# Moving the low parts of w1 from GpSimd to VectorE, one slice later, in a fused attention and two-MoE kernel

## The chip, the cores and the metric

The kernel runs on one core of one Trainium2 chip. The metric is the device time of one execution in microseconds (us). Five engines of the core work beside each other, each through its own instructions in order: TensorE (PE; its weight loads are shown as PEld), VectorE (DVE), ScalarE (ACT), GpSimd (POOL) and SyncE (SP), which issues most DMAs. An instruction starts when those ahead of it on its engine are through and the semaphores it waits for have been raised.

## The reference

Three layers follow each other. Only the second one matters here.

```python
x = attention(q, k, v)                      # 4 x 768 tokens, 512 wide: 3072 rows
logits = x @ w_gate                         # 8 experts
for idx in argsort(-logits.flatten()):      # greedy: best pair of token and expert first
    tok, e = divmod(idx, 8)
    if assigned[tok] >= 0 or counts[e] >= 384: continue
    assigned[tok] = e; counts[e] += 1
for e in range(8):                          # 384 tokens for each expert
    out[assigned == e] = relu(x[assigned == e] @ w1[e]) @ w2[e]
return soft_moe(out, phi, m2w1, m2w2)       # 32 slots, softmax over tokens and over slots
```

`w1[e]` is 512 x 1024 and `w2[e]` 1024 x 512, all in float32.

## The kernel before

**Stages.** After the attention the kernel finds, by a search, which expert fills first and with which 384 tokens, then the next, and so on: eight stages `r` = 0 to 7, one expert each. Here stage r.s means step s of stage r. While stage r multiplies, the search for later stages runs beside it.

**A step.** Stage r has 8 steps `fc`, one for each slice of 128 columns of w1. A step's product (`mm1`, L1251) is made of 12 matmuls of 128x384: x and w1 are both split into a high part in float32r and a low part (the rest), and high times high, high times low of x, and low of w1 times high are added. ScalarE then applies the relu (`hT`, L1262), and TensorE transposes (`turn_h`, L1272). `dispatch(r - 1)`, a generator, adds pieces of the finished stage's work at the ends of the steps: its fifth piece, at the end of step 4, multiplies by the first half of w2 (`pS`, L1430) and then issues the loads of the second half (`weights2`, L1240), since w2 has two buffers; the second half of `pS` stands at the end of step 6.

**Weights of a step.** SyncE loads a slice of w1 into `raw` (L1202, 256 KB, 4 buffers). ScalarE copies it, rounded, into `wh` (L1216), and GpSimd subtracts, `wl = raw - wh` (L1218; VectorE only for the first two slices of all). Both have 3 buffers. At the start of step k, `split` makes wh and wl of slice k + 2, and `fetch` issues the load of slice k + 6, which goes into the `raw` that slice k + 2 has used: SyncE waits there until that slice's wl is made. SyncE's other loads (w2, `pr`, and `mw`, the weights of the third layer) stand behind in the same queue.

**Other work of GpSimd** in these stages: three gathers of token rows for the next stage (L1171), and three scatters for the last (L1308).

**The search** (`_assign_rounds`) goes round by round, six digits each, back and forth between VectorE and TensorE. In the profile's lines: VectorE compares (`G`, L760) and prepares (`D1`, L767); TensorE counts (`A`, L791); VectorE casts (L800); TensorE picks (`B`, L803); VectorE (L814); TensorE adds (`C`, L816); VectorE (L819) and again L760. After the last digit VectorE makes `B_r` (L827), TensorE sums (`M`, L830 and L831), VectorE decides in nine small operations (L833 to L852), TensorE makes offsets (`o`, L700 and L701), and VectorE goes on (L856 to L869). `T` (L625) places tokens.

**What sets the order.** All engines follow the order in which the code is written. Where the search's instructions fall among the others is set by a running estimate: each matmul adds its cost to `pe` in `tick`; when `pe` reaches the time at which VectorE's answer should be ready, `advance` writes the search's next instructions, for TensorE and VectorE, at that place. `search_state["dve"]` estimates when VectorE is free; `other` adds VectorE work that isn't the search's. The subtraction on GpSimd does not stand in it.

Of the kernel before, what the change touches and what calls it, by code (L numbers as in the profile page):

```python
# [10 lines left out]
F32 = mybir.dt.float32  # L11
# [5 lines left out]
ALU = mybir.AluOpType  # L17
# [898 lines left out]
def tile_kernel(  # L916
# [13 lines left out]
    nc = tc.nc  # L930
# [17 lines left out]
    search_state = {"pe": 0.0, "dve": 0.0, "ready": 1e18, "cost": 0.0, "done": False, "stage": -1, "placed": set()}  # L948
# [204 lines left out]
    with ExitStack() as c2:  # L1153
        wp = c2.enter_context(tc.tile_pool(name="wp", bufs=2))

        XG, EI, ER, W, W2, PR, RAW = {}, {}, {}, {}, {}, {}, []
# [34 lines left out]
        def low_x():  # L1191

            dc, pt = LOW.pop(0)
            nc.vector.tensor_tensor(X[:, 1, dc], pt, X[:, 0, dc].bitcast(F32), ALU.subtract)
            other(480)

        def fetch(k):

            while len(RAW) <= k and len(RAW) < 8 * E and len(RAW) // 8 in EI:
                r, u = divmod(len(RAW), 8)  # L1200
                raw = ring.tile([128, 4, 128], F32, name=f"raw{r}_{u}", tag="raw", bufs=NRAW)
                nc.sync.dma_start(  # L1202
                    raw,
                    w1[bass.ds(number(r), 1), :, 128 * u : 128 * u + 128].rearrange("o (c p) f->p (o c) f", p=128),
                )
                RAW.append(raw)

        def split(k):

            fetch(k)  # L1210
            while len(W) <= k and len(W) < len(RAW):
                r, u = divmod(len(W), 8)
                raw = RAW[len(W)]
                wh = ring.tile([128, 4, 128], F32R, name=f"wh{r}_{u}", tag="wh", bufs=NWHL)
                wl = ring.tile([128, 4, 128], F32R, name=f"wl{r}_{u}", tag="wl", bufs=NWHL)
                nc.scalar.copy(wh, raw)  # L1216

                (nc.gpsimd if r or u > 1 else nc.vector).tensor_tensor(wl, raw, wh.bitcast(F32), ALU.subtract)  # L1218
                W[8 * r + u] = (wh, wl)

        def fetch_p(r):
            pr = wp.tile([128, 8, 32], F32, name=f"pr{r}", tag="pr", bufs=1)
            nc.sync.dma_start(
                pr.rearrange("p c s->p (c s)"), pd[bass.ds(number(r), 1), :, :].rearrange("o p s->p (o s)")
            )
            PR[r] = pr
# [233 lines left out]
        def part(t, i):  # L1460
            return lambda name: [t[:, 1024 * i : 1024 * i + 1024]]
# [21 lines left out]
        with tc.manual_schedule(engines=engines | {mybir.EngineType.Activation}):  # L1483
            for r in range(E):
                search_state["stage"] = r
                if r:
                    fetch_p(r)
                fill = dispatch(r - 1) if r else iter(())
                next(fill, None)
                for fc in range(8):  # L1490
                    split(8 * r + fc + NWHL - 1)
                    fetch(8 * r + fc + NWHL - 1 + NRAW)
                    if r == 0 and fc == 1:
                        fetch_p(r)
                    ahead = fc == 7 and r + 1 in XG
                    if ahead:
                        mm1(r, 7, (lambda: None, lambda: transpose_x(r + 1, 0), lambda: transpose_x(r + 1, 1), low_x))
                    elif fc == 4:
                        mm1(r, 4, (lambda: None, lambda: logits(r, 0)))
                    elif r == E - 1 and fc in (2, 3):  # L1500
                        mm1(r, fc, (lambda: None, lambda: next(fill)))
                    else:
                        mm1(r, fc)
                    if r == E - 1 and fc == 7:
                        logits(r, 1, range(3))
                    if fc == 2:
                        next(fill, None)
                    while turned < 8 * r + fc - (2 if 8 * r + fc < 8 * E - 3 else 1) + 1:
                        turn_h(*divmod(turned, 8))
                        turned += 1  # L1510
                    if ahead:
                        low_x()
                    if fc >= 3 and r + 1 in PLACED and r + 1 not in XG:
                        gather(r + 1)
                    if r == E - 1 and fc == 5:
                        weights2(r, (2, 3))
                    if fc != 2:
                        next(fill, None)
                    while early and NPRE - len(early) < (NPRE * (8 * r + fc)) // 56:
                        load_pieces(early.pop(0))  # L1520
                    if search_state["done"] and not late:
                        right.close()
                        late.append(right.enter_context(tc.tile_pool(name="late", bufs=NLATE, side="right")))
                        later += NLATE * [slot(late[0], "mw")]
                    if later and fc % 2:
                        load_pieces(later.pop())
                    if r == E - 1 and fc == 1:
                        load_pieces(part(xp.tile([128, 1536], F32, name="xg_mw", tag="xg"), 0))
                    if r == E - 1 and fc >= 6:
                        load_pieces(halves(ring, ("wh", "wl"), NWHL))  # L1530
                for _ in fill:
                    pass
                if r + 1 < E:
                    while r + 1 not in PLACED:
                        advance()
                    if r + 1 not in XG:
                        gather(r + 1)
                        until = search_state["pe"] + 5000
                        while search_state["ready"] < until:
                            advance()  # L1540
                        search_state["pe"] = max(search_state["pe"], until)
                    for dc in range(4):
                        if dc > 1 or not ahead:
                            transpose_x(r + 1, dc)
                            if len(LOW) > 1:
                                low_x()
                    while LOW:
                        low_x()
                    logits(r, 1)
                else:  # L1550
                    logits(r, 1, (3,))
                    turn_h(r, 7)
                    filler(r, 1)
            x = xp.tile([128, 3072], F32, name="x_mw", tag="x")
            load_pieces(halves(ring, ("wh", "wl"), NWHL), *[part(x, i) for i in range(3)])
            for _ in dispatch(E - 1):
                pass
            load_pieces(*2 * [slot(ring, "w2", 2)], *2 * [halves(ring, ("raw", "raw"), NRAW)])
# [200 lines left out]
```

## Time and profile before

| | us |
|---|---|
| median of 3 runs | 572.71 (572.52 to 573.27) |
| the profiled execution, its own time | 575.3 |
| its span, first to last instruction | 573.6 |
| stage 0 begins | 235.2 |
| stages 1, 2, 3, 4, 5, 6, 7 begin | 266.2, 303.0, 338.9, 376.6, 409.9, 441.7, 473.7 |
| last product of stage 7 ends | 500.2 |

The 1.7 us between span and time lie around the instructions. In the span TensorE is busy 93%, VectorE 60%, ScalarE 55%, GpSimd 38%. A row of a timeline gives the start and the duration in us, the engine, the line, the operation, what it writes and reads, shapes, and in square brackets how long the engine sat idle ahead of it and what ended that. Records of matmuls overlap: the next one starts before the record of the one ahead ends.

### The profile page before, as it was taken

To read this page: it belongs to the slowest core of one execution; us is meant where nothing else is said; L and a number is where in the kernel's file an instruction comes from. 1 tells how busy PE (TensorE), PEld (TensorE's weight loads), DVE (VectorE), ACT (ScalarE), POOL (GpSimd) and SP (SyncE) were. 2 spreads that over 40 slices of the span, in tenths; PEclk is the share of its full clock that TensorE was granted. 3 is DMA by queue.
4 is the path that set the end of the run, shared out by engine and by line. 5 is a ranking of instruction groups with operands and counts; after the bars stand their busy time and mean duration, and the time that the engine had idled before them with its cause. 6 is when DMAs were issued, how large, how long until landed. Compare 5 with 4: busy or idle time off the path is not lost.

```text
span 573.6 us, 15062 instructions
## 1 busy us (share of the span) xinstructions
PE 531.9 (93%) x5765; PEld 387.8 (68%) x5765; DVE 342.4 (60%) x1115; ACT 315.9 (55%) x670; POOL 219.0 (38%) x264
## 2 busy tenths in 40 slices
PE   4889999999998999998999999999999989979994
PEld 3676877777776766677667676677677767753473
DVE  5688987959845576879778897573423213031242
ACT  2778887878755766544536354455464535421231
POOL 3666554536410003153362554625465553421000
PEclk9999999999999999999999999999999999999998
DMA  9997896995865994355284674856859895789997
GB/s 188 202 192 185 221 193 160 250 232 167 311 209 193 392 332 147 102 169 171 94 289 147 200 252 127 264 173 208 281 160 342 252 338 170 250 260 370 357 346 215
DMA packets 157795, 130.64 MB, mean 228 GB/s; under 512 B 43332, under 2 KB 128964, under 8 KB 157724
## 3 DMA queue, kind: packets, MB, share of 16 engines
q1 hardware_dynamic: 151916, 115.26, 70.1%
q0 software_dynamic: 4368, 13.37, 7.3%
q10 hardware_dynamic: 1440, 1.05, 0.6%
q8 instruction: 46, 0.75, 0.6%
q14 instruction: 25, 0.20, 0.1%
HBM read 113.98 MB, written 14.02 MB: 223 GB/s over the span
## 4 chain that ended last, share of the span: by engine, by line
PE 61%; DVE 19%; DMA 6%; ACT 5%; issue 4%; POOL 3%; another core or an unknown queue 1%; SPq 0%; POOLq 0%; DVEq 0%; ACTq 0%
PE ph L1251 15%; DMA w<-in_moe_w_dram 5%; PE pwt L1049 4%; PE pp L1014 3%; PE po L1710 3%; PE pS L275 3%; PE po L313 3%; PE mh L1647 2%; PE pS L1430 2%; PE pt L1272 2%; DVE G_r L760 2%; PE l L1292 2%; PE pA L1325 2%; PE pf L1669 2%; PE pv L177 2%
## 5 line engine op out<-in xcount | busy, mean ns | idle before, releaser
L1251 PE MATMUL ph<-x,wh 128*128 128x384 f32 x512 | 145.6, 360 | 0.0
L1218 POOL TENSOR_TENSOR wl<-raw,wh 128x512 fp32r<-128x512 f32 x62 | 82.6, 1334 | 132.7 <-ACT wh L1216 104.4
L1251 PEld LDWEIGHTS ph<-x,wh 128*128 128x128 f32 x512 | 88.6, 189 | 22.2 <-issue 20.3
L1251 PE MATMUL ph<-x,wl 128*128 128x384 f32 x256 | 88.5, 346 | 0.0
L1262 ACT ACTIVATE hT<-ph 128x384 f32<-128x384 f32 x64 | 31.2, 488 | 74.7 <-PE ph L1251 63.2
L292 POOL TENSOR_TENSOR X<-X,mn 128x480 f32<-128x480 f32 x48 | 47.3, 985 | 64.2 <-DVE mn L288 40.2
L1251 PEld LDWEIGHTS ph<-x,wl 128*128 128x128 f32 x256 | 48.1, 188 | 0.0
L1171 POOL DMA_INDIRECT xg<-xd,ids x24 | 23.2, 968 | 61.6 <-PE pwt L1049 52.4
L287 DVE TENSOR_TENSOR X<-pS,nm 128x480 f32<-128x480 f32 x48 | 31.3, 651 | 14.8 <-PE pS L275 14.2
L1216 ACT CAST wh<-raw 128x512 fp32r<-128x512 f32 x64 | 39.9, 623 | 0.0
L1064 ACT COPY wt<-pwt 128x512 f32<-128x512 f32 x60 | 33.1, 591 | 11.8 <-PE pwt L1049 10.5
L221 ACT COPY kT<-pk 64x384 f32<-64x384 f32 x62 | 31.4, 507 | 9.8 <-PE pk L206 9.0
L1049 PE MATMUL pwt<-ident,pw 128*128 128x128 f32 x224 | 33.6, 281 | 1.1 <-ACT wt L1064 0.6
L296 ACT ACTIVATE X<-X 128x480 f32<-128x480 f32 x48 | 29.3, 610 | 8.4 <-POOL X L292 7.6
L1272 PE MATMUL pt<-ident,hT 128*128 128x128 f32 x192 | 33.9, 277 | 0.0
L275 PE MATMUL pS<-kwin,qT 64*64 64x120 f32 x768 | 32.1, 276 | 1.8 <-POOL kwin L243 1.8
L1274 ACT COPY h<-pt 128x384 f32<-128x384 f32 x64 | 30.2, 474 | 6.1 <-PE pt L1272 5.8
L288 DVE TENSOR_REDUCE mn<-X 128x4 f32<-128x480 f32 x48 | 31.3, 653 | 3.7
L275 PEld LDWEIGHTS pS<-kwin,qT 64*64 64x64 f32 x768 | 28.1, 138 | 5.0 <-POOL kwin L243 2.4
L1308 POOL DMA_INDIRECT cd<-ce,ids x24 | 24.5, 1020 | 17.5 <-DVE den L1422 13.6
L313 PEld LDWEIGHTS po<-vw,AT 120*64 120x64 f32 x768 | 24.9, 137 | 8.6 <-issue 3.1
L760 DVE TENSOR_TENSOR G_r<-D_r,as_cn 128x768 bf16<-128x768 bf16 (+1 forms) x41 | 29.2, 713 | 1.2
(293 smaller groups left out, 1062.1 us busy)
## 6 DMA issues: line engine op xcount, KB each, us to landing
mw<-in_moe_w_dram SPq DMA_DIRECT2D x55, 512.0 KB
raw<-in_moe_w_dram SPq DMA_DIRECT2D x64, 256.0 KB
w<-in_moe_w_dram SPq DMA_DIRECT2D x30, 512.0 KB
pw<-in_moe_w_dram SPq DMA_DIRECT2D x28, 512.0 KB
vw<-in_v_dram SPq DMA_DIRECT2D x32, 240.0 KB
kt<-in_k_dram SPq DMA_DIRECT2D x32, 192.0 KB
qt<-in_q_dram SPq DMA_DIRECT2D x32, 192.0 KB
xd<-xb POOLq DMA_DIRECT2D x4, 1536.0 KB
```

What stands on the lines that cost most here:

```text
L221: lambda r, d, s: nc.scalar.copy(d, s) if n or r else nc.vector.tensor_copy(d, s),
L275: nc.tensor.matmul(PS[n][i][64 * u : 64 * u + 64, j, :], qT[r, 64 * T : 64 * T + 64], kwin[r, T, :], start=True, stop=True,)
L287: nc.vector.tensor_tensor(X, PS[n][i], nm[:, i // 2], ALU.add)
L292: nc.gpsimd.tensor_tensor(X, X, MN.pop((n, i))[:, :, None].to_broadcast([128, 4, 120]), ALU.subtract)
L313: nc.tensor.matmul(PO[n][T // 6][64 * (T % 2) : 64 * (T % 2) + 64, T // 2 % 3, hh, :], AT[n, i][0:120, j, 64 * u : 64 * u + 64], vw[0:120, ...
L760: v.tensor_tensor(G, Dg.rearrange("p (q j)->p q j", j=J)[:, :, None, :].to_broadcast([128, 24 // J, n, J]), C["cn", n][:, None].to_broadca ...
L1049: nc.tensor.transpose(pt[:, dc], PW[e, q][t][:, 128 * dc : 128 * dc + 128], ident)
L1064: nc.scalar.copy(wt[:, :, 128 * t : 128 * t + 128], pt)
L1216: nc.scalar.copy(wh, raw)
L1218: (nc.gpsimd if r or u > 1 else nc.vector).tensor_tensor(wl, raw, wh.bitcast(F32), ALU.subtract)
L1251: nc.tensor.matmul(ph, a[:, dc], b[:, dc], start=dc == n == 0, stop=(dc, n) == (3, 2),)
L1272: nc.tensor.transpose(pt[:, c], HT[r, fc][:, 128 * c : 128 * c + 128], ident)
```

## The change

The subtraction of slice k + 2 is no longer issued with its copy. `split` puts it on a list, `WL`, and `low_w`, called at the start of each step, ahead of `split`, takes the oldest entry and issues it on VectorE. So at the start of step k VectorE gets wl of slice k + 1, and the copy of slice k + 2 follows on ScalarE. The first two slices are done at once, as before. Each call adds 600 ns to the estimate of VectorE. GpSimd keeps the gathers and scatters. Lines behind the edit are higher by 10 or 11 (L1251 is then L1261, L1430 is L1440, L1240 is L1250; the subtraction is L1228).

```diff
                 nc.scalar.copy(wh, raw)
-
-                (nc.gpsimd if r or u > 1 else nc.vector).tensor_tensor(wl, raw, wh.bitcast(F32), ALU.subtract)
                 W[8 * r + u] = (wh, wl)
+                WL.append((wl, raw, wh))
+                if r == 0 and u < 2:
+                    low_w()
+
+        WL = []
+
+        def low_w():
+
+            if WL:
+                wl, raw, wh = WL.pop(0)
+                nc.vector.tensor_tensor(wl, raw, wh.bitcast(F32), ALU.subtract)
+                search_state["dve"] = max(search_state["dve"], search_state["pe"] + 196) + 600
...
                 for fc in range(8):
+                    low_w()
                     split(8 * r + fc + NWHL - 1)
```

TensorE before, from the end of 1.4 into 1.5 (`ph1_4` and `ph1_5` are the products of the two steps, `pt` a transpose, `pS0` the first half of the second product, `as` the search's bank):

```order
L830 MATMUL as_3045<-as_w23_483,as_on_487 128x8
L831 LDWEIGHTS as_o32_319
L831 MATMUL as_3045<-B_r3_4964,as_o32_319 128x8
L1251 MATMUL ph1_4_4954<-x_3023,wl1_4_4792 128x384
L1251 MATMUL ph1_4_4954<-x_3023,wh1_4_4791 128x384 x2
L1251 MATMUL ph1_4_4954<-x_3023,wl1_4_4792 128x384
L1272 MATMUL pt1_2_5004<-ident_66,hT1_2_4836 128x128 x3
L1430 MATMUL pS0_0_5013<-w2_0_0_4093,aT0_4941 32x512 x2
L1430 MATMUL pS0_0_5013<-w2_0_1_4095,aT0_4941 32x512 x2
L1251 MATMUL ph1_5_5030<-x_3023,wh1_5_4878 128x384 x2
L700 LDWEIGHTS as_tri_840
```

And changed, at the same place:

```order
L803 MATMUL as_3045<-c4_r3_4960,as_pk32_653 128x8
L1282 MATMUL pt1_2_4984<-ident_66,hT1_2_4805 128x128 x3
L1440 MATMUL pS0_0_4993<-w2_0_0_4093,aT0_4915 32x512 x2
L1440 MATMUL pS0_0_4993<-w2_0_1_4095,aT0_4915 32x512 x2
L830 LDWEIGHTS as_on_487
L830 MATMUL as_3045<-as_w23_483,as_on_487 128x8
L831 LDWEIGHTS as_o32_319
L831 MATMUL as_3045<-B_r3_4979,as_o32_319 128x8
L1261 MATMUL ph1_5_5029<-x_3023,wh1_5_4861 128x384 x2
```

M, the sum that VectorE's nine small operations wait for, has moved from ahead of the first half of pS to right behind it; in 2.4 and 3.4 of the changed kernel it stands in the middle of that half.

VectorE before, the end of the nine operations behind M and what follows, in 1.4 and 1.5:

```order
L689 SCALAR_TENSOR_TENSOR cur_r3_4993<-as_go_854,V_r3_4988 128x48
L852 TENSOR_TENSOR x1_r3_4995<-go_r3_4986,dE_s3_4784 128x24
L856 SCALAR_TENSOR_TENSOR tie_r3_5035<-V_r3_4988,cur_r3_4993 128x24
L857 SCALAR_TENSOR_TENSOR gone_3046<-V_r3_4988,gone_3046 128x24
L859 TENSOR_TENSOR D0_s3_4782<-D0_s3_4782,x1_r3_4995 128x24
```

And changed (`wl1_6` is the low part of slice 6 of stage 1):

```order
L689 SCALAR_TENSOR_TENSOR cur_r3_5013<-as_go_854,V_r3_5008 128x48
L852 TENSOR_TENSOR x1_r3_5015<-go_r3_5006,dE_s3_4822 128x24
L1228 TENSOR_TENSOR wl1_6_4924<-raw1_6_4617,wh1_6_4923 128x512
L856 SCALAR_TENSOR_TENSOR tie_r3_5049<-V_r3_5008,cur_r3_5013 128x24
L857 SCALAR_TENSOR_TENSOR gone_3046<-V_r3_5008,gone_3046 128x24
```

The subtraction now stands behind the last of the nine operations, and the search's next ones behind it.

SyncE before, at the end of 1.4, with the semaphores that each load waits for (`raw2_2` is slice 2 of stage 2, `w2_0_2` and `w2_0_3` the second half of stage 0's w2):

```order
L1202 DMA raw2_2_4952<-in_moe_w1_dram 128x4x128 [waits DMAHW0_49,Pool_49]
L1240 ISA
L1240 DMA w2_0_2_5018<-in_moe_w2_dram 128x2x512 [waits DMAHW7_49,PE_49]
L1240 ISA
L1240 DMA w2_0_3_5020<-in_moe_w2_dram 128x2x512 [waits PE_49]
L1147 DMA mw5_5022<-in_moe2_w1_dram 128x2x512 [waits DMAHW1_49]
```

And changed:

```order
L1202 DMA raw2_2_4926<-in_moe_w1_dram 128x4x128 [waits DMAHW0_49,DVE_49]
L1250 ISA
L1250 DMA w2_0_2_5017<-in_moe_w2_dram 128x2x512 [waits DMAHW7_49,PE_49]
L1250 ISA
L1250 DMA w2_0_3_5019<-in_moe_w2_dram 128x2x512 [waits PE_49]
L1147 DMA mw5_5021<-in_moe2_w1_dram 128x2x512 [waits DMAHW1_49]
```

The order is the same; the load of `raw2_2`, which takes the buffer of slice 6 of stage 1, now waits for VectorE instead of GpSimd, and the two w2 loads stand behind it.

## Rows read from the trace of the kernel before

**Rows 1.** TensorE's waits in stages 0 to 4: us in total, times, longest
```profile
PE as L791 <- DVE G_r L760: 4.3, 9, 1.1
PE as L803 <- DVE c_r L800: 3.0, 6, 0.8
PE as L830 <- DVE B_r L827: 1.1, 2, 0.6
```
**Rows 2.** Timeline, step 1.5, TensorE
```profile
290.08 0.51 PE L1251 MATMUL ph<-x,wh 128*128 128x384 f32 x2
```
**Rows 3.** Groups of instructions, whole span: busy us, mean ns | idle before, releasers
```profile
L1251 PE MATMUL ph<-x,wh 128*128 128x384 f32 x512 | 145.6, 360 | 0.0
L1218 POOL TENSOR_TENSOR wl<-raw,wh 128x512 fp32r<-128x512 f32 x62 | 82.6, 1334 | 132.7 <-ACT wh L1216 104.4 <-DVE G_r L760 11.9 <-PE pt L1272 11.4
L1218 DVE TENSOR_TENSOR wl<-raw,wh 128x512 fp32r<-128x512 f32 x2 | 1.3, 683 | 0.0
```
**Rows 4.** Timeline, stage 0, VectorE and GpSimd
```profile
256.32 3.14 DVE L861 SCALAR_TENSOR_TENSOR D_s<-V_r,D_s 128x24 f32<-128x24 f32 x1
256.89 2.52 POOL L1218 TENSOR_TENSOR wl<-raw,wh 128x512 fp32r<-128x512 f32 x2
```
**Rows 5.** Line 767: duration ns min/median/max, first and last start us
```profile
L767 DVE TENSOR_SCALAR D_r<-D_r x41: 164/171/1260, 185.8 to 388.7; 128x24 f32<-128x24 bf16 x41
```
**Rows 6.** Groups of VectorE, stages 0 to 4 (columns as in Rows 3)
```profile
L767 DVE TENSOR_SCALAR D_r<-D_r 128x24 f32<-128x24 bf16 x28 | 11.3, 403 | 0.0
L819 DVE SCALAR_TENSOR_TENSOR D_r<-D_r,as,E_r 128x24 bf16<-128x24 f32 x24 | 11.0, 458 | 11.9 <-PE as L816 9.0 <-PE as L625 2.8
L861 DVE SCALAR_TENSOR_TENSOR D_s<-V_r,D_s 128x24 f32<-128x24 f32 x4 | 5.3, 1324 | 0.0
```
**Rows 7.** Timeline, step 1.6, a wait of TensorE for the search
```profile
293.27 0.46 PE L791 MATMUL as<-O_b,G_r 128*128 128x16 bf16 x12 [0.23 <-DVE G_r L760]
```
**Rows 8.** Timeline, TensorE, both halves of pS in stages 1, 2, 3, 6
```profile
288.30 1.06 PE L1430 MATMUL pS<-w,aT 128*32 128x512 f32 x8
295.64 2.18 PE L1430 MATMUL pS<-w,aT 128*32 128x512 f32 x8
324.33 1.06 PE L1430 MATMUL pS<-w,aT 128*32 128x512 f32 x8
331.84 1.66 PE L1430 MATMUL pS<-w,aT 128*32 128x512 f32 x8
360.75 1.07 PE L1430 MATMUL pS<-w,aT 128*32 128x512 f32 x8
...
370.64 1.04 PE L1430 MATMUL pS<-w,aT 128*32 128x512 f32 x2
458.22 1.07 PE L1430 MATMUL pS<-w,aT 128*32 128x512 f32 x8
...
467.97 1.05 PE L1430 MATMUL pS<-w,aT 128*32 128x512 f32 x4 [0.30 <-DMA w<-in_moe_w_dram]
```
**Rows 9.** Timeline, SyncE's issues of w2's second half in stages 1, 2, 3, 6
```profile
289.40 0.95 SPq L1240 DMA_DIRECT2D w<-in_moe_w_dram  x2
325.80 0.95 SPq L1240 DMA_DIRECT2D w<-in_moe_w_dram  x2
362.17 0.95 SPq L1240 DMA_DIRECT2D w<-in_moe_w_dram  x2
459.57 0.37 SPq L1202 DMA_DIRECT2D raw<-in_moe_w_dram  x1
460.20 0.99 SPq L1240 DMA_DIRECT2D w<-in_moe_w_dram  x2
```
**Rows 10.** Timeline, step 1.4, from M to the last of the nine operations
```profile
287.06 0.17 PE L831 MATMUL as<-B_r,as_o 128*128 128x8 bf16 x1
...
288.66 0.15 DVE L852 TENSOR_TENSOR x_r<-go_r,dE_s 128x24 f32<-128x24 bf16 x1
```
**Rows 11.** Line 1171, gathers: duration ns min/median/max, first and last start us
```profile
L1171 POOL DMA_INDIRECT xg<-xd,ids x24: 942/960/1062, 222.4 to 457.3; - x24
```

## The prediction

> **What bounds the kernel now.** I read the page first: TensorE is busy 93% of the span, so a change pays only where TensorE waits. I then took its waits in stages 0 to 4 (235.17 to 409.90 us), the only stages in which both the search and the subtraction on GpSimd run. There TensorE waits for VectorE in the search: 4.3 us for G, 3.0 for the cast, 1.1 for B_r, 8.4 us in 17 waits [rows 1]. That is too little by what overlapping records hide: a product's record lasts 0.36 us [rows 3], but two of them in a row take 0.51 [rows 2], so the next could start 0.15 to 0.17 after the first, and each wait began some 0.16 earlier than the idle time shows. 17 × 0.16 = 2.7: **about 11.1 us of TensorE waiting for the search.**
>
> Next, why VectorE is late. In the timeline an operation of 24 elements, L861, takes 3.14 us; it ends at 259.46, just when two subtractions on GpSimd end (256.89 + 2.52 = 259.41) [rows 4]. L767 takes 0.17 us as a rule and 1.26 at worst [rows 5], which is about one subtraction on GpSimd, 1.33 [rows 3]. So small operations of the search stand still while GpSimd subtracts. In stages 0 to 4 L767 means 403 ns in place of 171: 28 × 0.23 = 6.5 us. L819 means 458; taking 0.25 for it, about what an operation of its size takes undisturbed, 24 × 0.21 = 5.0. L861 means 1324 against some 170: 4 × 1.15 = 4.6 [rows 6]. Three lines carry 16 us of stretched time, on the very chain for which TensorE waits.
>
> The third view is SyncE's queue and pS. The second half of w2 is loaded in two pieces, issued when the first half of pS has freed its buffers, and TensorE waits for the landing at the second half: it takes 2.18 us in stage 1 against 1.06 undisturbed [rows 8]. This wait exists in stages 1 to 6, 0.6 to 3.7 us each.
>
> **What is removed.** 62 subtractions leave GpSimd. GpSimd's own time is worth nothing, since it idles 132.7 us ahead of them [rows 3]. What counts is that VectorE is no longer held up. All but a few short ones of the 17 waits have a stretched operation in front, so I let the 11.1 us go, except those that lie between the two halves of pS, where the w2 load ends last anyway: one in stage 1 (0.23) [rows 7], two in stage 2 (0.33, 0.17), one in stage 3 (0.45), with the hidden part 1.2 + 4 × 0.16 = 1.8. **Gain 9.3 us.** Bounds: 6 if a third of the waits have other causes, 11.1 if none is covered.
>
> **What is added on VectorE.** 62 × 0.683 us = 42 us [rows 3], 5.5 a stage. In stages 0 to 4, 42 slices × 0.683 = 29 us. Against that stand the 16 us of the three lines and single stretched operations on a dozen others, so VectorE is about as full as before. The difference is that the estimate counts these (600 each), and places the search's matmuls later, where before it knew nothing of the stretches. The search then runs up to one step later against the products, but its gathers still come two steps before the transposes that need them, so nobody waits for its end. An estimate that is 83 ns short for each slice, on the fifth or so that stand right ahead of a search matmul, gives about 0.7 us of new waits.
>
> A product needs its wl one step after VectorE gets it. A step lasts at least 2.35 us; the subtraction and the queue ahead of it usually take less. The tight place is 1.5 to 3.5: the nine operations end 288.81 − 287.06 = 1.75 us behind M [rows 10], wl of slice 6 is ready 0.68 later, 2.4 us behind M, and slice 6 needs it some 3.2 us behind. Cover 0.8 us. I put 0.3 us for places where it fails; bounds 0 and 4. New waits together **−1.0 us.** From stage 5 on VectorE has little to do and this is hidden.
>
> **What is moved on SyncE.** This is the cost. The load of raw (r+1, 2) stands ahead of w2's second half. It waits for wl of slice 6, which GpSimd used to make during step 4, and VectorE now makes at the start of step 5, behind M's nine operations. Call T the end of the first half of pS: 289.36, 325.39, 361.82 in stages 1 to 3 [rows 8]. Before, w2 was issued at T + 0.04, T + 0.41, T + 0.35 [rows 9]. Now M stands at T in stage 1 and at T − 0.5 in stages 2 and 3; add 1.75, 0.68, and 0.63 from the start of the raw load to that of w2 (459.57 to 460.20) [rows 9]: T + 3.1, T + 2.6, T + 2.6. From the first issue to the end of the second half passed 8.4 us in stage 1 (297.82), 7.7 in stage 2 (333.50), 9.5 in stage 3 (371.68), and 8.8 in stage 6 (469.02) [rows 8, 9]. In stage 3 a search matmul held up the end; without it some 7.9. All of these waited for the load, so the load sets them; I take 7.9. Then the second half ends at T + 11.0, 10.5 and 10.5 instead of T + 8.5, 8.1 and 9.9: **−5.5 us**. With 7.0, as in stage 4, the shortest of the six, it is −2.9; with 8.8, −8.2.
>
> In stage 4 M comes after wl of slice 6, and only B_r is ahead: w2 goes out about 0.85 us later. In stage 5 an addition that waits for ScalarE is ahead, 0.3 us. In stage 6 nothing is ahead: GpSimd had put the raw load at 459.57, 0.28 behind T (459.29), and w2 at T + 0.9 [rows 8, 9]; now VectorE makes wl in step 4, and w2 goes out at T: +0.9. Together **−0.25 us**. The other loads (w2's next first half, pr, mw) are used many steps later; the later raw loads still have about 11 us to spare.
>
> **The sum.** 9.3 − 1.0 − 5.5 − 0.25 = 2.5 us. The profiled execution took 575.3 us, which becomes 572.8; it was 2.6 us above the median of the runs, 572.71, so the forecast is **570.2 us**. A measurement of this kernel can tell about 0.2%, 1.1 us, from no change.
>
> **The rivals.**
>
> *The w2 load costs more than the search gains: slower.* For it: all six stages already wait at the second half, so any delay of that issue is paid in full; the shared queue can't be passed. Against it: the search's waits are as plain. With 8.8 us from issue to end: 8.2 in stages 1 to 3, some 2.6 in stage 4 (T + 1.1 + 8.8 against T + 7.3), 0.5 in stage 5, nothing won in stage 6, 1.0 for new waits: 9.3 − 12.3 = −3.0, or 575.7 us. It decides from a loss of 2.8 us a stage in stages 1 to 3, that is, if w2 is issued 3.5 us or more behind T, or lands a microsecond slower. Chance 0.23.
>
> *VectorE is simply too full: products wait for wl.* If half of the 24 steps of stages 1 to 3 wait 0.4 us, 5 us are lost on top, 572.7 + 2.5 = 575.2 us. Against it: the cover above. Chance 0.06.
>
> *No change.* The search waits as before, since VectorE's load is the same, and the wait is only placed elsewhere, so half the gain is missing: 9.3 becomes 5 to 7, and the sum lies within 1 us of zero, 572.5 us. Chance 0.16.
>
> *Everything is won.* The loads land as fast as in stage 4 (7.0), and the waits vanish whole: 11.1 − 1.0 − 2.9 + 0.5, and up to 2 more if TensorE catches up search work while it waits at pS: some 9 us, 563.7. For it: while TensorE stands at pS, VectorE empties its queue. Chance 0.15.
>
> *The hold-up turns round.* VectorE's subtraction could hold up GpSimd as GpSimd's held up VectorE: three gathers a stage, 0.96 us each [rows 11], 0.68 later each, 2 us later in all. If the next stage's transposes then waited 1 us in each of five stages, the forecast becomes 575.2. Against it: the gathers' durations spread by only 0.12 us beside a busy VectorE [rows 11], and they end well ahead of their use. Chance 0.03.
>
> The Trainium skill says in "SBUF — State Buffer" (Who interferes with whom) that VectorE and GpSimd share one pair of ports, that whichever instruction starts first keeps it to its end, and that a VectorE instruction with two SBUF inputs collides with a GpSimd instruction that reads SBUF. By that rule the last rival is possible, at the price just given. Rows 4 agree with it for the direction from GpSimd to VectorE; no row shows the other with a price.
>
> **How the numbers follow.** The forecast, a small gain, has the rest, 0.37, with its own range of 566 to 572. Faster by over 0.2%: most of the forecast and all of "everything is won", 0.54. Within 0.2%: the lower edge of the forecast and most of "no change", 0.18. Slower: the first two rivals, most, and the last, 0.28. The range leaves out 1 in 10 on either side: from 563.0, just under "everything is won", to 577.0, beyond the first rival by the 1.3 us that further waits for wl could add.
>
> **What the profile of the changed kernel would show.** L767, L819 and L861 with means near 0.17, 0.25 and 0.17 us; otherwise the hold-up has another cause. Idle time ahead of L791, L803 and L830 falling from 8.4 to under 3 us; if not, VectorE's fullness was the cause. SyncE's w2 issues in stages 1 to 3 some 2.6 to 3.1 us behind the first half of pS, and the idle time ahead of the second half growing by 5 us; if w2 goes out at once, I misread the queue, and the time is nearer 564. No waits of L1261 for L1228. The prediction fails most likely in the time from w2's issue to its landing, which depends on what else is in the queues.

## The result and the profile after

The changed kernel takes **582.04 us** (median; 577.16 to 584.64) where the kernel before takes 573.72 (six runs, among them the three reported above): a ratio of **1.015 (95% interval 1.0115 to 1.0186), slower**, though by less than 2%. The forecast was 570.2 with a range of 563.0 to 577.0; the time lies above the range, on the other side of no change. The profiled execution took 581.98 us with a span of 580.0, against 575.3 and 573.6 before.

The gain that the prediction speaks of is there. The longest waits of TensorE in stages 0 to 7 of the changed kernel, of which none is for the search (line waited at, releaser: us in total, times, longest):

```profile
PE pS L1440 <- DMA w<-in_moe_w_dram: 9.2, 5, 3.6
PE px L1186 <- DMA xg<-xd,ids: 4.5, 3, 2.2
PE px L1186 <- ACT h L1284: 2.0, 3, 0.9
...
```

The three lines of [rows 1], 8.4 us for the search, are gone. Others stand in their place: 9.2 us at the second half of pS for w2, 4.5 us at the transpositions of x for the gather, and 2.0 us at transpositions of x for ScalarE's copies, in steps 1.7, 2.7 and 3.7. Of these the kernel before has only the first, and less of it, in the same view:

```profile
PE pS L1430 <- DMA w<-in_moe_w_dram: 3.1, 4, 2.3
```

VectorE's groups in stages 0 to 4 (busy us, mean ns | idle before) and line 861 (duration ns min/median/max) answer to [rows 3, 6]:

```profile
L819 DVE SCALAR_TENSOR_TENSOR D_r<-D_r,as,E_r 128x24 bf16<-128x24 f32 x24 | 5.9, 248 | 13.5 <-PE as L816 10.7 <-PE as L625 2.6
L767 DVE TENSOR_SCALAR D_r<-D_r 128x24 f32<-128x24 bf16 x28 | 4.8, 171 | 0.0
...
L861 DVE SCALAR_TENSOR_TENSOR D_s<-V_r,D_s x4: 173/173/175, 257.5 to 373.0; 128x24 f32<-128x24 f32 x4
```

So the stretching was GpSimd's doing: means of 403, 458 and 1324 ns fell to 171, 248 and 173.

The losses stand in two places. The first is the end of stage 0, GpSimd's gathers for stage 1 and TensorE's transpositions of them:

```profile
255.03 0.94 POOL L1171 DMA_INDIRECT xg<-xd,ids  x1 [28.79 <-PE as L831]
...
257.56 0.97 POOL L1171 DMA_INDIRECT xg<-xd,ids  x1 [0.30 <-issue]
...
259.45 0.30 PE L1186 MATMUL px<-ident,xg 128*128 128x128 f32 x1 [1.07 <-DMA xg<-xd,ids]
261.96 0.48 PE L1186 MATMUL px<-ident,xg 128*128 128x128 f32 x1 [2.21 <-DMA xg<-xd,ids]
263.68 0.47 PE L1186 MATMUL px<-ident,xg 128*128 128x128 f32 x1 [1.25 <-DMA xg<-xd,ids]
```

The second is w2 in stages 1 to 3. SyncE's queue: the raw load (it stands 0.62 us ahead in all three stages), then the two issues of w2's second half:

```profile
293.06 0.37 SPq L1202 DMA_DIRECT2D raw<-in_moe_w_dram  x1
293.68 0.95 SPq L1250 DMA_DIRECT2D w<-in_moe_w_dram  x2
...
333.40 0.95 SPq L1250 DMA_DIRECT2D w<-in_moe_w_dram  x2
...
373.23 0.95 SPq L1250 DMA_DIRECT2D w<-in_moe_w_dram  x2
```

TensorE in the same stages, the end of the first half of pS with M beside it, and the second half with its wait:

```profile
289.65 1.07 PE L1440 MATMUL pS<-w,aT 128*32 128x512 f32 x8
...
290.69 0.17 PE L831 MATMUL as<-B_r,as_o 128*128 128x8 bf16 x1
...
298.97 1.92 PE L1440 MATMUL pS<-w,aT 128*32 128x512 f32 x4 [3.06 <-DMA w<-in_moe_w_dram]
...
301.24 1.42 PE L1440 MATMUL pS<-w,aT 128*32 128x512 f32 x4
...
330.41 0.17 PE L831 MATMUL as<-B_r,as_o 128*128 128x8 bf16 x1
330.51 1.05 PE L1440 MATMUL pS<-w,aT 128*32 128x512 f32 x4
...
338.76 1.17 PE L1440 MATMUL pS<-w,aT 128*32 128x512 f32 x4 [1.73 <-DMA w<-in_moe_w_dram]
340.12 1.92 PE L1440 MATMUL pS<-w,aT 128*32 128x512 f32 x4 [0.19 <-DMA w<-in_moe_w_dram]
...
380.47 3.52 PE L1440 MATMUL pS<-w,aT 128*32 128x512 f32 x8 [3.62 <-DMA w<-in_moe_w_dram]
```

Eight of these products take 1.07 us at 289.65 and 3.52 at 380.47: not only the wait, but the work behind it is longer. A table of stages (window, us, busy time and instructions of PE, PEld, DVE, ACT and POOL, granted clock, DMA share, GB/s) shows why. First stage 0 of the kernel before, whose clock is 1.00 in every stage, then stages 0 to 3 of the changed kernel:

```profile
235.17:266.16 30.99, 27.78 (x228) 21.98 (x226) 26.60 (x96) 15.07 (x33) 13.15 (x10) 1.00 0.52 163
```

```profile
235.37:269.38 34.01, 29.49 (x226) 23.46 (x224) 22.07 (x99) 15.14 (x33) 2.89 (x3) 0.90 0.47 148
269.38:308.32 38.94, 35.31 (x289) 25.08 (x285) 27.30 (x122) 17.38 (x39) 6.67 (x9) 0.96 0.52 165
308.32:348.15 39.83, 37.06 (x285) 25.66 (x281) 26.61 (x116) 17.43 (x40) 7.21 (x9) 0.96 0.59 186
348.15:389.98 41.83, 37.04 (x285) 25.41 (x281) 26.67 (x119) 18.32 (x42) 7.21 (x9) 0.96 0.54 175
```

The records put the granted clock at 0.5, the level of 1.2 GHz, for 6.83 us from 261.06 (stage 0, during the wait for the gather) and for 3.41 us each from 298.60, 339.56 and 380.52 (at the waits for w2 or right behind them). Lengths of the stages, from first product to first product, and from the last product to the end, in the profiled executions (us):

| kernel | 0 | 1 | 2 | 3 | 4 | 5 | 6 | 7 | rest |
|---|---|---|---|---|---|---|---|---|---|
| before | 31.0 | 36.9 | 35.9 | 37.8 | 33.3 | 31.8 | 32.0 | 26.5 | 73.4 |
| changed | 34.0 | 38.9 | 39.8 | 41.8 | 34.4 | 29.2 | 29.3 | 26.6 | 70.7 |

Stages 0 to 4 lose 14.3 us, stages 5 and 6 win 5.3, the rest wins 2.8.

### The profile page after: what moved, and what is told of

It is laid out like the page before. It is cut to its first block, busy times and chain, and to the rows that moved or that the text cites. A ratio compares the mean times of both kernels' runs of the same rounds, so it can differ in the third digit from the quotient of the medians.

```text
span 580.0 us, 15029 instructions
## 1 busy us (share of the span) xinstructions
PE 539.4 (93%) x5765; PEld 391.4 (67%) x5765; DVE 346.8 (60%) x1177; ACT 315.4 (54%) x670; POOL 140.3 (24%) x202
## 3 DMA queue, kind: packets, MB, share of 16 engines
q10 hardware_dynamic: 1440, 1.05, 0.6%
## 4 chain that ended last, share of the span: by engine, by line
PE 68%; DVE 13%; DMA 7%; ACT 4%; POOL 3%; SPq 3%; issue 2%; DVEq 0%; POOLq 0%; ACTq 0%
PE ph L1261 22%; PE pS L1440 4%; DMA w<-in_moe_w_dram 4%; PE pwt L1049 4%; PE pp L1014 3%; PE pt L1282 3%; PE po L1721 3%; PE l L1302 3%; PE mh L1658 2%; PE pA L1335 2%; DVE mn L288 2%; DVE X L287 2%; PE px L1186 2%; SPq L91 2%; PE pS L275 2%; PE pf L1680 2%
## 5 line engine op out<-in xcount | busy, mean ns | idle before, releaser
L1261 PE MATMUL ph<-x,wh 128*128 128x384 f32 x512 | 145.8, 360 | 0.0
L1261 PEld LDWEIGHTS ph<-x,wh 128*128 128x128 f32 x512 | 89.2, 190 | 24.3 <-issue 20.8
L1261 PE MATMUL ph<-x,wl 128*128 128x384 f32 x256 | 88.5, 346 | 0.0
L1228 DVE TENSOR_TENSOR wl<-raw,wh 128x512 fp32r<-128x512 f32 x64 | 43.7, 685 | 16.3 <-ACT wh L1216 16.0
L1261 PEld LDWEIGHTS ph<-x,wl 128*128 128x128 f32 x256 | 48.4, 189 | 0.0
L1318 POOL DMA_INDIRECT cd<-ce,ids x24 | 26.4, 1101 | 58.9 <-DVE ce L1395 30.9
L1440 PE MATMUL pS<-w,aT 128*32 128x512 f32 (+1 forms) x144 | 29.0, 612 | 9.2 <-DMA w<-in_moe_w_dram 9.2
L1187 ACT CAST x<-px 128x384 fp32r<-128x384 f32 x32 | 14.7, 487 | 39.6 <-PE px L1186 39.6
L296 ACT ACTIVATE X<-X 128x480 f32<-128x480 f32 x48 | 29.3, 610 | 8.8 <-POOL X L292 8.3
```

The lines of the kernel that those rows point to most:

```text
L1228: nc.vector.tensor_tensor(wl, raw, wh.bitcast(F32), ALU.subtract)
L1261: nc.tensor.matmul(ph, a[:, dc], b[:, dc], start=dc == n == 0, stop=(dc, n) == (3, 2),)
L1440: nc.tensor.matmul(pS[32 * g : 32 * g + 32, cols], aT[:, fc % 2, 32 * (fc // 2) : 32 * (fc // 2) + 32], W2[r, fc // 2][fc % 2][:, cols], s ...
```

## The experiments

Each group of four runs was made on one chip, beside the kernel before. The chips differ, the changed kernel among them more than the kernel before (last section), so runs are compared by their ratio to the kernel before, or within a group. Theory at the start: the search's later place in the order costs stage 0 through the gather, the raw load in front of w2 costs stages 1 to 3, and each long wait adds a stretch of low clock. Rivals: VectorE is too full; the queues of the DMAs are; the waits cover what the clock takes.

### First group: the two causes taken away

**The raw loads one step later**, so that the load ahead of w2 in SyncE's queue is one whose buffer is free:

```
-  fetch(8 * r + fc + NWHL - 1 + NRAW)
+  fetch(8 * r + fc + NWHL - 2 + NRAW)
```

> The changed kernel, with the load of each raw slice asked for one step later, so that raw (r+1, 1), whose buffer is free in step 4, and not raw (r+1, 2) stands ahead of the second half of w2 in SyncE's queue. Theory (the loss in stages 1 to 3 is w2 held behind that raw load, plus the low clock that each of these waits brings on): w2 goes out within 0.7 us behind the first half of pS; the waits of 3.06, 1.73 and 3.62 us at the second half in stages 1 to 3 shrink to under 1 us each and the three stretches of 3.41 us at clock 0.5 vanish; stage 0 keeps its wait of 4.5 us for the gather; 566 to 571 us in place of 582. Rival (w2 is slow because gathers and other loads share its DMA queues): w2 goes out earlier but lands little earlier; 578 to 582 us.

Measured: 566.53 us, ratio 0.990 (0.987 to 0.9924). The waits of TensorE in stages 0 to 7:

```profile
PE px L1186 <- DMA xg<-xd,ids: 4.2, 3, 2.6
...
```

No line for w2 is left; it goes out as soon as its buffers are free (0.03 us behind the first half of pS in stage 1), and the stretches of low clock in stages 1 to 3 are gone (that of stage 0 remains). The steps with the second half, 1.6, 2.6 and 3.6, take 4.95, 4.51 and 4.98 us where the changed kernel took 9.34, 7.89 and 10.01. The theory holds: the raw load ahead of w2 was what held it. Against the first run of the changed kernel, made apart from this group, the edit is worth 15.5 us; the third run shows how much of that is VectorE's doing.

**No estimate for the low parts**, the search in the order of the kernel before:

```
   nc.vector.tensor_tensor(wl, raw, wh.bitcast(F32), ALU.subtract)
-  search_state["dve"] = max(search_state["dve"], search_state["pe"] + 196) + 600
```

> The changed kernel without the line that adds 600 to the running estimate for each low part: the search stands between the products as in the kernel before, the low parts stay on VectorE. Theory (the estimate is what puts the search one step later, and with it the gather of stage 1): the wait of 4.5 us for xg in step 0.7 and the 6.8 us at clock 0.5 behind it vanish, some 7 to 8 us; w2 stays late in stages 1 to 3; some waits for the search return, at most 4 us, since nothing holds VectorE up any more; 574 to 578 us. Rival (VectorE is too full, and the estimate only showed it): TensorE waits for the search 8 to 11 us in stages 0 to 4, as before; 580 us or more.

Measured: 565.60 us, ratio 0.988 (0.9843 to 0.9913), better than expected. The waits of TensorE in stages 0 to 7:

```profile
PE pS L1439 <- DMA w<-in_moe_w_dram: 4.4, 7, 1.2
PE as L803 <- DVE c_r L800: 0.8, 3, 0.4
PE as L791 <- DVE pr_r L637: 0.4, 1, 0.4
...
PE px L1186 <- DMA xg<-xd,ids: 0.3, 1, 0.3
PE as L700 <- DVE tot_r L687: 0.3, 1, 0.3
PE as L791 <- DVE G_r L760: 0.2, 1, 0.2
```

Stage 0 takes 27.7 us. The waits for the search stay away although nothing keeps them away by order: 1.7 us in all, so VectorE is not too full. I had expected w2 to stay as late as in the changed kernel. It comes earlier: in the old order M stands 2.3 to 7.7 us ahead of the end of the first half of pS, so that VectorE has M behind it when low part 6 is due, and w2 goes out 0.7, 2.2 and 0.6 us behind that end (in stage 2 low part 6 is itself late, by 1.6). No stretch of low clock is left in any stage.

**The kernel before with later raw loads** (the same edit as in the first experiment, GpSimd still makes the low parts):

> The kernel before, with the same later raw loads as in the changed kernel with loads one step later. Theory: there the second half of w2 went out at 0.04 to 0.9 us behind the first half of pS, so moving the raw load is worth at most 1.5 us: 571.5 to 573.5 us, the same as before. Rival (the raw load ahead of w2 costs by its bytes in the DMA queues, not by its wait): 3 us or more faster here too, 569 us or less.

Measured: 566.52 us, ratio 0.989 (0.9854 to 0.9934). My theory fell and the rival held. The waits of TensorE in stages 0 to 7:

```profile
PE as L791 <- DVE G_r L760: 5.1, 8, 1.3
PE as L803 <- DVE c_r L800: 4.2, 6, 1.3
PE as L830 <- DVE B_r L827: 1.2, 2, 0.6
...
```

The waits for w2 are gone, those for the search are all there. In stage 5 w2 is issued 0.03 us behind the first half in both, but the second half ends 6.21 us behind it in place of 7.72: before, the last raw load had started 0.7 us ahead of w2, here it is out of the way. So the kernel before paid for that raw load too, and in stage 5 not by a wait: by its bytes, as I read it.

The changed kernel with the same edit took 566.53 us on this chip: with the raw loads out of the way the two kernels are level. In that pair the changed kernel's stage 0 is 2.8 us longer, and its stages 1, 2, 5 and 6 are 4.1 us shorter together. So some 7 of the 15.5 us are what the edit gives the kernel before too. The other 8, by this comparison of two sittings, about as much as the whole loss, are the price of the raw load's wait for VectorE, with the low clock behind it.

**Both edits to the changed kernel:**

> The changed kernel with both: raw loads one step later and no estimate for the low parts. Theory: both losses go, and the search's waits of 8.4 us stay mostly away, so that 560 to 565 us are left, faster than the kernel before by 1.5% or more. Rival (VectorE too full without the estimate): the search's waits return, 569 to 574 us.

Measured: **560.95 us, ratio 0.978 (0.9745 to 0.9814)**, faster than the kernel before on this chip, and than the changed kernel in any of its runs, though that was not run on this chip. The waits of TensorE in stages 0 to 7:

```profile
PE px L1186 <- DMA xg<-xd,ids: 1.7, 1, 1.7
PE pS L1439 <- DMA w<-in_moe_w_dram: 1.4, 3, 0.6
...
```

Set against the run above, which has the same order of search and loads and differs in who makes the low parts, the move to VectorE alone is worth 5.6 us. In the two traces stages 0 to 4 take 167.9 in place of 172.9 us: 9 us less waiting for the search, 3 more for xg and w2.

### Second group: the order, the lag and the clock

**Products that nobody reads in the waits**, to keep TensorE at work there:

```
+  def warm(n):                    # a PSUM tile, n products of the identity
...
   yield
   yield
+  if r < 3:
+      warm((24, 12, 28)[r])       # ahead of the second half of pS
...
+  if (r, dc) == (1, 0):
+      warm(34)                    # ahead of the transpositions for stage 1
```

> The changed kernel with products of the identity that nobody reads, put where TensorE stands: 24, 12 and 28 ahead of the second half of pS in stages 1, 2 and 3 (14 such lasted 1.72 us, so 2.9, 1.5 and 3.4 us) and 34 (4.2 us) ahead of the first transposition for stage 1. Nothing that anyone waits for comes earlier by it. Theory (the waits bring on the low clock, which costs as much again as half of each stretch): the stretches at clock 0.5 in stages 0 to 3 (6.83 and three of 3.41 us) vanish, and the time falls by 6 to 8.5 us, to 573.5 to 576 us. Rival (the work in these stretches is covered by the waits for loads anyway): 580 to 583 us, though the clock stays up.

Measured: 594.96 us, ratio 1.029 (1.0209 to 1.0377). Inconclusive: theory and rival had both put less. A product took 0.228 us, twice what I had reckoned from the timeline, where each shows as two records. The 34 lasted 7.75 us and ended some 2 us behind the wait they were to fill. The clock did stay up in stages 0 to 3. The third group repeats it with fewer.

**The 600 only from stage 1 on:**

```
+  if search_state["stage"] > 0:
       search_state["dve"] = max(search_state["dve"], search_state["pe"] + 196) + 600
```

> The changed kernel, with the 600 added only from stage 1 on: in stage 0 the search stands as in the kernel before, and from step 1.1 on as in the changed kernel. Theory (stage 0 loses to the late gather alone, and stages 1 to 3 to the search's later place and w2): stage 0 falls from 34.0 to about 28 us, stages 1 to 3 keep 38 to 42 us each with their stretches at clock 0.5; 575 to 577 us. Rival (an early start lets the search run ahead for the rest): stages 1 to 3 as without the estimate, 36 us each, 566 us.

Measured: 588.84 us, ratio 1.018 (1.0103 to 1.0266). Stage 0 takes 28.0 us, stages 1 to 3 take 40.6, 38.6 and 41.5, with a low clock in stages 1 and 3 and none in stage 2; that is near what I expected. The time is not, and on this chip can't be set beside the changed kernel. So it was run again, below.

**Without the lag of one slice**, each low part right behind its high part:

```
   WL.append((wl, raw, wh))
-  if r == 0 and u < 2:
-      low_w()
+  low_w()
```

> The changed kernel without its one slice of delay: each low part is made by VectorE right behind the copy of its high part, still counted as 600. Low part 6 then stands in step 4, ahead of M's operations. Theory (w2 is held by low part 6 behind M): w2 goes out within 1 us behind the first half of pS, stages 1 to 3 take 35 to 37 us each in place of 39 to 42, no stretch at clock 0.5 there; stage 0 keeps its wait for the gather; 566 to 571 us. Rival (a full VectorE, wherever the low part stands in its queue): the waits at the second half stay, 578 us or more; or products wait for wl.

Measured: 591.02 us, ratio 1.022 (1.0142 to 1.0303). Half of it came out. Low part 6 is now done 3.3 us ahead of M, w2 goes out as soon as its buffers are free, and steps 1.6, 2.6 and 3.6 take 4.95, 4.88 and 4.86 us: it is low part 6 behind M that holds w2. But the search has moved back further, and waits again. TensorE's waits in stages 0 to 4:

```profile
...
PE as L803 <- DVE c_r L800: 5.6, 5, 1.6
...
PE as L791 <- DVE G_r L760: 2.0, 5, 0.8
...
```

Stage 0 takes 39.1 us, 10 of them at the low clock. Stages 1 to 3 take 38.9, 37.9 and 38.2, not the 35 to 37 I had put, and stage 1 has a stretch of 3.41 us at the low clock. As I read it, the lag is what gives the search its place ahead of the low parts on VectorE.

**The order alone**: the kernel before, GpSimd makes the low parts, the estimate counts them:

```
+  search_state["dve"] = max(search_state["dve"], search_state["pe"] + 196) + 600
   W[8 * r + u] = (wh, wl)          # in split, of the kernel before
```

> The kernel before, with GpSimd still making the low parts, and only the estimate raised by 600 for each: the order of the changed kernel alone (one step later than that in stage 0, the same from stage 1). Theory: the gather of stage 1 comes late and costs 4 to 7 us in stage 0 with a stretch at clock 0.5; the search's waits fall from 8.4 to under 4 us; w2 is not held by VectorE; 573 to 578 us. Rival 1 (the order alone makes the loss): 580 us or more. Rival 2 (the order does no harm without VectorE's extra work): 570 us or less.

Measured: 582.00 us, ratio 1.0062 (1.0024 to 1.01). By its time it would speak for the first rival, but the kernel before took 579.3 us on this chip. Stage 0 takes 34.1 us with 6.83 at the low clock, and in stages 1 to 3 w2 goes out as soon as its buffers are free, both as expected. The search's waits come to 5.2 us, where I had put under 4.

### Third group: beside the changed kernel

> The changed kernel as it is, timed and profiled beside the next three, since two chips differed by some 5 us for the kernel before too. Every theory expects a ratio to the kernel before of about 1.015, stage lengths of 34, 39, 40 and 42 us in stages 0 to 3, and stretches at clock 0.5 in these four stages.

Measured: 593.46 us, ratio 1.0307 (1.0257 to 1.0357): on this chip the changed kernel loses twice as much. Stages 0 to 3 take 34.1, 41.3, 38.5 and 42.2 us; the low clock stands in stages 0, 1 and 3, not in stage 2.

**The unread products again**, 13, 7, 15 and 20:

> The changed kernel with the same unread products as in the run with 24, 12, 28 and 34 of them. There one took 0.228 us and not 0.12, so that they outlasted the waits. Now 13, 7 and 15 ahead of the second half of pS (3.0, 1.6 and 3.4 us) and 20 (4.6 us) ahead of the transpositions for stage 1. Theory (the low clock behind a wait costs): 1.8 us less in stage 0 and about 1.3 in each of stages 1 to 3, 4 to 6 us less than the changed kernel on the same chip. Rival (covered): within 1.5 us of the changed kernel.

Measured: 588.80 us, ratio 1.023 (1.0174 to 1.0286), **4.7 us less than the changed kernel**. The windows of stages 0 to 3, first the changed kernel on this chip, then this one (columns as above, the granted clock third from the end):

```profile
234.98:269.08 34.10, 29.48 (x225) 23.57 (x223) 22.17 (x99) 15.15 (x33) 2.89 (x3) 0.90 0.47 148
269.08:310.35 41.27, 36.59 (x289) 25.73 (x285) 27.39 (x122) 17.50 (x39) 6.68 (x9) 0.92 0.51 161
310.35:348.86 38.51, 35.61 (x285) 25.31 (x281) 26.63 (x116) 17.54 (x40) 7.20 (x9) 1.00 0.58 185
348.86:391.08 42.22, 38.59 (x286) 27.20 (x282) 26.64 (x119) 18.43 (x42) 7.21 (x9) 0.92 0.59 193
```

```profile
235.09:266.71 31.62, 31.46 (x265) 26.14 (x263) 22.06 (x99) 14.92 (x33) 2.89 (x3) 1.00 0.51 160
266.71:305.26 38.55, 36.95 (x314) 27.91 (x311) 27.31 (x122) 17.48 (x39) 6.67 (x9) 1.00 0.52 166
305.26:343.99 38.73, 37.31 (x300) 26.91 (x296) 26.62 (x116) 17.41 (x40) 7.21 (x9) 1.00 0.60 189
343.99:383.49 39.50, 38.34 (x315) 28.69 (x311) 26.63 (x119) 18.30 (x42) 7.20 (x9) 1.00 0.58 188
```

Where the clock had been 0.90 or 0.92, a stage is 2.5 to 2.7 us shorter; in stage 2, where it had been 1.00 anyway, nothing changes (+0.2). These stages win 7.7 us in the traces; some 3 of them are lost again in stage 6 and behind the last product. Work was added and time fell, so the low clock costs by itself, and the rival falls.

**The 600 only from stage 1 on, again:**

> The 600 added only from stage 1 on, now beside the changed kernel. Theory: stage 0 about 28 us in place of 34, all other stages within 1.5 us of the changed kernel's; 4.5 to 7 us less than the changed kernel on the same chip. Rival: what stage 0 wins is lost again in stages 1 to 4; within 2 us of it.

Measured: 587.96 us, ratio 1.022 (1.0167 to 1.0273), 5.5 us less than the changed kernel. Stage 0 takes 27.7 in place of 34.1 us, the wait for xg is down from 4.6 to 0.3; stage 1 takes 2.4 us less, the others stay within 0.7, and what follows the last product takes 2.4 more. The order of stage 0 alone is worth what was expected.

**The order alone, again:**

> The changed kernel's order with GpSimd still making the low parts, now beside the changed kernel. Theory: the same late gather in stage 0 (34 us), but w2 goes out at once, so stages 1 to 3 take 37 to 38 us each and not 39 to 42; 4 to 8 us less than the changed kernel on the same chip, and within 3 us of the kernel before. Rival (the order alone makes the whole loss): within 2 us of the changed kernel.

Measured: 581.07 us, ratio 1.0101 (1.0047 to 1.0155): **12.4 us less than the changed kernel, and about 5 more than the kernel before**. Its waits in stages 0 to 4:

```profile
PE as L803 <- DVE c_r L800: 3.5, 4, 1.4
PE px L1186 <- DMA xg<-xd,ids: 2.9, 3, 1.2
...
PE as L791 <- DVE G_r L760: 1.9, 4, 0.6
...
```

Stages 0 to 3 take 33.3, 37.7, 37.2 and 37.9 us. So the later order makes the kernel slower by itself, but not by the whole loss, and by more than the 3 us I had allowed. Stage 0 is where it shows most (33.3 us with 3.41 at the low clock, 31.0 in the profile of the kernel before, from another sitting); in stages 1 to 3 it needs the low part on VectorE as well to hold w2. I had expected 4 to 8 us; 6.5 of the 12.4 lie in stages 4 and 5, where the changed kernel takes 7.6 us more on this chip than at first.

## Why the prediction was wrong

**The views and the cause of the search's waits: right.** L767, L819 and L861 fell to 171, 248 and 173 ns as put, and the idle time ahead of L791, L803 and L830 went from 8.4 us to none. The gain of 9.3 us is too high as a net price. With the search and the loads in the same order, the waits for the search fall from 10.5 to under 2 us, some 3 us of other waits appear, and the time falls by 5.6.

**The step that failed first, and by most,** is the sentence that the search "then runs up to one step later against the products, but its gathers still come two steps before the transposes that need them, so nobody waits for its end". I counted in steps and not in microseconds. The third gather for stage 1 and the first transposition, before:

```profile
255.92 0.95 POOL L1171 DMA_INDIRECT xg<-xd,ids  x1 [0.30 <-issue]
...
261.63 0.49 PE L1186 MATMUL px<-ident,xg 128*128 128x128 f32 x3
```

That is a cover of 5.7 us. In the changed kernel the gather starts at 257.56, 1.6 later, and TensorE stands at the transposition at 259.45 − 1.07 = 258.38, 3.2 us earlier, because the search no longer holds it up: before, four waits for the search, 2.7 us of idle time, stood ahead of it in stage 0. The cover is 0.8 us, where the three gathers take 4.3 to 6.1 us from issue to landing. The gain itself used up two thirds of what the gather lost of its cover. Stage 0, which wins 3.3 us in the old order (27.7), lost 3.0: 6.3 us that the sum did not have. Giving stage 0 its old order brings 5.5 us back on the chip where both ran.

The later place has a second price that the sum put at nothing: the 2.0 us of transpositions that wait for ScalarE's copies in steps 1.7, 2.7 and 3.7. All runs with the later order in these stages have them (2.0 to 2.3 us), also with GpSimd making the low parts; the four kernels with the old order have none. In step 1.7 of the profile of before a search product stands there (L791, at 301.08).

**The w2 step was right in the mechanism and mis-sized in the price.** w2 was put at T + 3.1, 2.6 and 2.6 us; it went out at T + 2.96, 1.84 and 1.84. In stages 2 and 3 M stands between the products of the first half, 1.15 us ahead of T and not 0.5; from M to the issue it is 3.0 us in all three, as worked out (1.75 + 0.68 + 0.63). From the issue to the end of the second half I took 7.9 us; it was 8.98, 8.65 and 10.76. What I left out is the clock. Four of these products take 1.05 us at full clock; in the second halves four of them took 1.92 and 1.42 in stage 1 and 1.92 in stage 2, and eight took 3.52 in stage 3: some 1.2, 0.9 and 2.5 us more. Without that, 7.7, 7.8 and 8.3 us are left, close to the 7.9. So the second half ends at T + 11.9, 10.5 and 12.6 where it ended at T + 8.5, 8.1 and 9.9: 8.6 us in place of 5.5, of which the clock is 4.6, while the earlier issue gave 1.7 back. The prediction had no term for a clock that falls; the profile of before, with 1.00 in every stage, showed none.

**The other loads of SyncE.** Stage 4 lost 0.7 at w2 (0.85 put). In stages 5 and 6 the sum had −0.3 and +0.9; they won 2.6 and 2.7 us. The row that I read as GpSimd's lateness, raw at 459.57 ahead of w2 at 460.20 [rows 9], was more than that: the kernel before with the later raw loads wins 1.5 and 2.8 us in these two stages, where its lateness was 0 and 0.9. I had priced the raw load by its wait alone. The Trainium skill says in "DMA: Bandwidth & Descriptors" (Two DMAs through the same engine are not ordered) that within one queue of a DMA engine descriptors start in order. The run is in keeping with it: with w2 issued at the same place, the second half ended 1.5 us sooner when no raw load had just gone in front. The order inside a DMA queue itself no trace here shows.

**New waits for wl: right.** No product of a step waited for L1228, in any stage.

**The rivals.** "The w2 load costs more than the search gains" was right in place and sign; at 575.7 us it lacked the clock and stage 0. "The hold-up turns round" named the right wait, transpositions waiting for the gather, with the wrong cause: the gathers last 943 to 1242 ns, median 968, against [rows 11] 942 to 1062, median 960. They are late because M stands later and TensorE comes to them sooner. By the rule of the Trainium skill in "SBUF — State Buffer" (Who interferes with whom), the order of issue decides which of two colliding instructions blocks the other. The gathers agree: the two that began while a subtraction ran took 1.24 and 1.22 us, the five in which a subtraction began 0.95 to 0.98. No transposition waited for the two, so this rival was worth nothing here. Rows 4, which the prediction called in agreement with the rule, show the collision but not that order: L861 is recorded from 256.32, ahead of the subtractions at 256.89, and still ended with them. "VectorE is simply too full" is refuted by the run without the estimate.

**What stays open.** The 2.8 us that the changed kernel wins behind the last product are a single stall in the profile of before, which the last section shows; it has nothing to do with the change, as far as the traces tell. How the rest of the loss in stages 1 to 3 splits between the later order and the low part on VectorE isn't settled to the microsecond, because either remedy alone frees w2. Nor is it known why the gathers take so long to land: six of them took 3.3 to 3.6 us in the kernel before with later raw loads.

## What to carry to other kernels

Where an order is set by running estimates, an operation that is moved to an engine moves all that the estimate of that engine places: work out the new slack of every transfer that hangs on it in microseconds, with the time that the gain itself takes away from it. An issue queue is one line: look at which wait stands ahead of an urgent load, and take it out of the way first (here that edit alone made the kernel before faster by 1%, and brought the changed kernel level with it; the move gained, by 5.6 us, once the estimate was taken out as well). A wait of some microseconds on TensorE costs more than its length when the granted clock falls in it.

## What the runs showed of the hardware

TensorE's clock. In the profile of the kernel before it stays at 1.00 through all stages, with waits of up to 2.3 us. In the changed kernel waits of 4.5 us (in three pieces) and of 3.06, 1.73 (with a second one of 0.19) and 3.62 us went with stretches at 0.5 of 6.83 and three times 3.41 us. On the chip of the third group the wait in stage 2, 1.75 us, went without one. Filling the waits with unread products took the stretches of stages 0 to 3 away and 4.7 us off the time.

GpSimd and VectorE. A subtraction on GpSimd stretched small operations of VectorE: in the mean from 171 to 403, from 248 to 458 and from 173 to 1324 ns. The other way round, a gather on GpSimd that began while VectorE subtracted took about 0.25 us longer (1.22 and 1.24 us, median 0.97).

Chips differ, and the granted clock is a part of that at most. The same changed kernel took 582.0 us at first, where the record names no chip, and 593.5 on the chip of the third group, at mean clocks of 0.977 to 0.985 and of 0.973 to 0.974; the kernel before took 573.7, 573.6, 579.3 and 576.0, at 0.989 to 0.995 on the chip of the first group and 0.984 to 0.993 on the other two. In every profile from the second and third group VectorE and ScalarE stall at the same two instructions in the end, with a releaser that the trace calls remote, and in some at others too. The profile of the kernel before has the two stalls in its end, the runs of the first group have none. First the kernel before, then the changed kernel in the third group (timeline, idle time before and releaser in brackets):

```profile
514.50 0.48 DVE L1443 SCALAR_TENSOR_TENSOR acc<-acc,al,pS 128x256 f32<-128x256 f32 x1 [3.17 <-remote]
```

```profile
297.87 0.49 ACT L1272 ACTIVATE hT<-ph 128x384 f32<-128x384 f32 x1 [3.64 <-remote]
```

The one at 297.87 falls into the wait for w2 in stage 1, whose step takes 10.89 us (9.34 at first). It does not make that wait: in the run with the short unread products, which has no such stall, the second half begins 9.12 us behind the end of the first, against 9.29. What these stalls are, the traces don't tell. They are a reason to set runs of one chip beside each other only.
